# Rows' root on VectorE and ScalarE, first pieces in halves and two products interleaved at the start of a Fourier and SwiGLU kernel

## The chip, the cores and the metric

One core of one Trainium2 chip. The metric is the device time of one execution in microseconds (us). Beside three timed runs there is one profiled execution, whose trace gives every instruction of the five engines (PE is TensorE, with PEld for its weight loads; DVE is VectorE; ACT is ScalarE; POOL is GpSimd; SP is SyncE, which only issues DMAs) and the DMA traffic. Times in the trace count from the start of its span.

## What is computed

```python
def reference(A_x, A_dft_seq_re, A_dft_seq_im, A_dft_hid_re, A_dft_hid_im, B_x, B_w_gate, B_w_up, B_w_down):
    xn = layernorm(A_x)                       # S=2048 rows, D=640
    a = einsum("bsd,ed->bse", xn, dft_hid_re)
    b = einsum("bsd,ed->bse", xn, dft_hid_im)
    s = einsum("ts,bse->bte", dft_seq_re, a) - einsum("ts,bse->bte", dft_seq_im, b)
    g = silu((silu(xn @ w_gate) * (xn @ w_up)) @ w_down)      # F=1536
    return A_x + s * g
```

All is float32.

## The kernel before

**Arithmetic.** Each float32 product is done as three matmuls in the reduced float32r format (`mm3`, lines 199 to 205): an operand is split into a high part (ScalarE, `high`, line 182) and a low part, the remainder (VectorE, `low`, lines 187 and 189), and high x high, high x low and low x high are added in PSUM. The three lines 203, 204, 205 are those three matmuls; the first needs both high parts, the second also the low part of the moving operand, the third the low part of the stationary one. Nearly all of TensorE's time is in them, 4290 matmuls.

**Stages.** First the Fourier transform along the sequence, four times (`seq(0)` to `seq(3)`: two pairs of column blocks, real and imaginary), then twice the transform along the hidden dimension (`hid`), gate and up (`gate_up`) and down (`down`). The sequence products use a Strassen scheme on quarters of the DFT matrix and of the normalised rows. In `seq` (line 526) the products are run in the order p1, d, p5, p2, p6, p3, p7, p4 for the first one. Each product has four blocks g = 0 to 3; a block takes one piece of 128x1024 of the DFT matrix (two tiles of 128x512) as moving operand S, and two row tiles of the normalised input as stationary operand T. A block of p1 and of p2 has 18 matmuls (two banks of p and a third for a fifth block of columns, called d1 or d2), a block of d has 6 (only the fifth column block, with the quarter a21), one of the others 12.

**Names used below.** x0 to x15 are the row tiles of x (128x640); x0 to x7 are loaded by SP for p1, x8 to x15 by GpSimd's queue for p2 (`load_x`, line 401). c0 to c3 are the four pieces of quarter 11 that p1 reads; R0 to R3 those of quarter 21 that d reads (`load`, line 546, on SP). Into R0 to R3 GpSimd's queue then adds quarter 22, with DMAs that accumulate (`accumulate`, line 551), which gives p5's operands; then quarter 11, for p6, and quarter 12, for p3. An accumulate may only start when the split of what was there before has been read.

**Normalisation of rows** (only `seq(0)`, `layer_norm`, line 403). For each pair of row tiles: two `bn_stats` per tile and one `bn_aggr` on VectorE (lines 410 and 412), then the inverse root of the variance, refined by one Newton step, on tiles of 128x2 (lines 420 to 435), then on ScalarE one activation per tile that scales and shifts it in place (line 440). For the first pair the small operations run on VectorE, with ScalarE's square root; for the seven other pairs on GpSimd, with `pow`: eight operations each, in GpSimd's queue, which also issues the accumulating DMAs and the loads of x8 to x15. After that T of the pair is split: high parts of 128x512 and 128x256 for the two p tiles and the d tile, low parts the same. p5, p6 and p4 use sums of row tiles made on VectorE (lines 459 and 478).

**What sets the order.** Nothing is scheduled at run time: `Plan` records every operation with a planned time, which is that of the product that needs it less a lead (`prod`), and raises it to what its reads and writes allow. All operations are then sorted by this time, and each engine executes its own in that order, waiting where a semaphore says so. The leads of the first sequence product stand in `LEAD` (line 522). `Plan.place` gives each buffer a place in two arenas by the planned lifetimes. An SP or GpSimd queue also waits, before its ninth DMA, for the first one's landing, and so on.

Ahead of the first product 16 matmuls on zeros (line 987) run on TensorE.

Of the kernel before, what the change touches and what calls it, by code (L numbers as in the profile page):

```python
# [13 lines left out]
P = 128  # L14
# [12 lines left out]
class Plan:  # L27
# [43 lines left out]
    def place(self, limits):  # L71
# [9 lines left out]
        for arena, limit in limits.items():  # L81
# [13 lines left out]
            where |= min(found, key=lambda f: f[0])[1]  # L95
# [3 lines left out]
    def fit(mine, limit, pauses):  # L99

        placed, where, cost = [], {}, 0.0
        for n, size, ta, ia, tb, ib in mine:
# [17 lines left out]
            for a, e, xa, ja, xb, jb in near:  # L120
                if a < o + size and o < e:
                    cost += max(0.0, 5 - (ta - xb if ta >= xa else xa - tb)) ** 2
            placed.append((o, o + size, ta, ia, tb, ib))
        return cost, where
# [3 lines left out]
def tile_fnet_swiglu(  # L128
# [27 lines left out]
    sm = one.tile([P, 6, NS], F32, name="sm")  # L156
# [246 lines left out]
    def layer_norm(k0, n, lead, root, stats, small):  # L403
# [4 lines left out]
        for k in range(k0, k0 + n):  # L408
            for h in range(2):
                pl.prod(stats, lambda k=k, h=h: nc.vector.bn_stats(  # L410
                    bst[:, k % 2, h], raw(xn, k * D + h * 320, 320)), [(xn, k)], [("bst", k % 2, h)])
            pl.prod(stats, lambda k=k: nc.vector.bn_aggr(
                mv[:, k], bst[:, k % 2].rearrange("p a b -> p (a b)")),
                [("bst", k % 2, 0), ("bst", k % 2, 1)], [("mv", k)])
        v, y, t, mr, nm, power = (sm[:, i, k0:k0 + n] for i in range(6))
        r = rowst[:, 0, NS + k0:NS + k0 + n]
        key = ("sm", k0)
        if small is nc.vector:
            ops = [
                lambda: small.tensor_scalar(v, mv[:, k0:k0 + n, 1], EPS, 1.0, op0=ALU.add, op1=ALU.mult),  # L420
                lambda: nc.scalar.activation(t, v, AF.Sqrt),
                lambda: small.reciprocal(y, t),
            ]
        else:
            ops = [
                lambda: small.tensor_scalar(v, mv[:, k0:k0 + n, 1], EPS, 1.0, op0=ALU.add, op1=ALU.mult),  # L426
                lambda: small.tensor_tensor(y, v, power, op=ALU.pow),  # L427
            ]
        ops += [
            lambda: small.tensor_scalar(nm, mv[:, k0:k0 + n, 0], -1.0, 0.0, op0=ALU.mult, op1=ALU.add),  # L430
            lambda: small.tensor_tensor(t, v, y, op=ALU.mult),
            lambda: small.tensor_tensor(t, t, y, op=ALU.mult),
            lambda: small.tensor_scalar(t, t, -0.5, 1.5, op0=ALU.mult, op1=ALU.add),
            lambda: small.tensor_tensor(r, y, t, op=ALU.mult),
            lambda: small.tensor_tensor(mr, nm, r, op=ALU.mult),
        ]
        for fn in ops:
            pl.prod(root, fn, [("mv", k) for k in range(k0, k0 + n)], [key])
        for k in range(k0, k0 + n):
            pl.prod(lead, lambda k=k: nc.scalar.activation(  # L440
                raw(xn, k * D, D), raw(xn, k * D, D), AF.Identity, bias=sm[:, 3, k:k + 1], scale=rowst[:, 0, NS + k:NS + k + 1]),
# [45 lines left out]
    def down_operands():  # L487

        for g in range(2):
# [32 lines left out]
    LEAD = {"S": (10, 8), "T": (14, 13, 11), "p1": (5.5, 0.6), "p5": (4.5, 2.5), "p2": (8, 6),  # L522
            ("d", 0): (8.8, 4.5), ("d", 1): (9.7, 5.7), ("d", 2): (8, 6.4), ("d", 3): (9.2, 7.7),
            "Tp1": (0, 2, 0), "Td1": (0, 2, 0), "Tp5": (5.5, 4.5, 2.6), "Tp2": (0, 6, 4), "Td2": (0, 6, 4)}

    def seq(k):
# [4 lines left out]
        top = {}  # L531
# [11 lines left out]
        def load(q, g, lead):  # L543
            seq.n += 1
            name = pl.buf(("c", seq.n), "raw", 2 * TC)
            pl.prod(lead, lambda: nc.sync.dma_start(wide(raw(name)), source(q, g)), [], [(name, 0)])
            return name

        def accumulate(name, q, g, lead):

            pl.prod(lead, lambda: nc.gpsimd.dma_start(wide(raw(name)), source(q, g), accum_op=ALU.add), [], [(name, 0)], 8)  # L551
# [5 lines left out]
        def operand(p, g, name):  # L557
            s = pl.buf(("S", k, p, g), "hl", 4 * TC)
            high, low = LEAD.get((p, g), LEAD.get(p, LEAD["S"])) if fresh else LEAD["S"]
            split(high, s, 2 * TC, lambda: raw(name), [(name, 0)], low_lead=low)  # L560
            return s

        def right_operand(p, g, per):

            width = P if p[0] == "d" else 256
            sums, high, low = LEAD.get("T" + p, LEAD["T"]) if fresh else LEAD["T"]
            view, keys = right(p, per * g // 4, sums)
            name = pl.buf(("T", k, p, per * g), "hl", 2 * per * width)
            at = per * g % 4
            split(high, name, per * width, lambda: view(at, per), keys[at:at + per] if len(keys) > 1 else keys,  # L570
                  scale=-1.0 if p == "p1" else None, low_lead=low)
            for i in range(per):
                top[p, per * g + i] = name, per, i, width

        def tw(p, kk, e):
            name, per, i, width = top[p, kk]
            return lambda part: hl(name, part, i * width + e * P, P)

        def run(p, left, banks, direct=None):

            per = 6 * (len(banks) + (direct is not None))
            operands = []
            rights = ([p] if banks else []) + ([f"d{direct[1]}"] if direct else [])
            start = pl.now
            for g in range(4):
                pl.now = start + g * per * MM
                operands.append(left(g))
                for r in rights:
                    few = 2 if fresh and r in ("p1", "d1", "p2", "d2") else 4
                    if (r, 2 * g) not in top:  # L590
                        right_operand(r, 2 * g // few, few)
            pl.now = start
            for g, s in enumerate(operands):
                todo = []
                reads = both(s)
                for kk in (2 * g, 2 * g + 1):
                    m = lambda i, kk=kk, s=s: hl(s, i, kk % 2 * TC, TC)
# [431 lines left out]
```

## Time and profile before

| what | us |
|---|---|
| three timed runs: median (lowest to highest) | 998.49 (998.20 to 999.53) |
| profiled execution, its own time | 999.22 |
| its span, first to last instruction | 997.2 |
| first matmul of p1, first of p5 | 11.93, 42.40 |
| mean granted clock of TensorE over the span | 0.994 |

The page gives busy time per engine and groups of instructions by source line. A line such as L182 or L187 is that of a helper, and stands for all splits; which operand a row belongs to follows from its place in the engine's order. `hl<-raw` is a split, `raw<-in_cs` a load or accumulate of the DFT matrix, `raw<-in_x` a load of rows. Rows of the timeline are: start, duration, engine, line, operation, shape, count, and in brackets how long the engine stood before and what ended that. A matmul of 512 columns shows 0.39 us, but they overlap; one starts every 0.226 us.

### The profile page before, as it was taken

To read this page: it belongs to the slowest core of one execution; us is meant where nothing else is said; L and a number is where in the kernel's file an instruction comes from. 1 tells how busy PE (TensorE), PEld (TensorE's weight loads), DVE (VectorE), ACT (ScalarE), POOL (GpSimd) and SP (SyncE) were. 2 spreads that over 40 slices of the span, in tenths; PEclk is the share of its full clock that TensorE was granted. 3 is DMA by queue.
4 is the path that set the end of the run, shared out by engine and by line. 5 is a ranking of instruction groups with operands and counts; after the bars stand their busy time and mean duration, and the time that the engine had idled before them with its cause. 6 is when DMAs were issued, how large, how long until landed. Compare 5 with 4: busy or idle time off the path is not lost.

```text
span 997.2 us, 11758 instructions
## 1 busy us (share of the span) xinstructions
PE 981.2 (98%) x4306; PEld 806.8 (81%) x4306; DVE 708.3 (71%) x912; ACT 499.4 (50%) x708; POOL 123.4 (12%) x204
## 2 busy tenths in 40 slices
PE   7899999999999999999999999999999999999998
PEld 4688888888888888888888888888888888887887
DVE  6787767946785686466678887787668666666686
ACT  6676554655375454424655555434434544445342
POOL 4760211001101010001111110000010100000000
PEclk9899999999999999999999999999999999999999
DMA  9879667656765776833545534489950311205683
GB/s 343 208 158 251 237 154 158 211 181 147 158 211 200 169 171 212 281 137 118 184 144 217 203 145 159 172 293 356 333 170 28 124 36 53 79 1 188 228 281 126
DMA packets 71193, 180.09 MB, mean 181 GB/s; under 512 B 6432, under 2 KB 22048, under 8 KB 71136
## 3 DMA queue, kind: packets, MB, share of 16 engines
q1 hardware_dynamic: 56064, 122.96, 36.3%
q0 software_dynamic: 15072, 56.39, 20.9%
q8 instruction: 33, 0.54, 0.2%
q14 instruction: 24, 0.20, 0.1%
HBM read 145.75 MB, written 33.57 MB: 180 GB/s over the span
## 4 chain that ended last, share of the span: by engine, by line
PE 89%; POOL 3%; DMA 3%; DVE 3%; issue 2%; ACT 1%; SPq 0%; POOLq 0%; DVEq 0%; ACTq 0%
PE ps L203 30%; PE ps L205 29%; PE ps L204 29%; DVE hl L187 1%; DMA p_dram<-raw 1%; POOL raw L551 1%; DMA raw<-in_cs 1%; DMA raw<-in_x 1%; DVE bst L410 1%; POOL sm L427 1%; ACT hl L182 0%; POOL sm L426 0%; POOL raw L401 0%; DVE raw L459 0%; POOL sm L430 0%
## 5 line engine op out<-in xcount | busy, mean ns | idle before, releaser
L203 PE MATMUL ps<-hl 128*128 128x512 f32 (+1 forms) x1430 | 558.3, 390 | 9.1 <-ACT hl L182 8.1
L204 PE MATMUL ps<-hl 128*128 128x512 f32 (+1 forms) x1430 | 557.5, 390 | 0.2 <-DVE hl L187 0.2
L205 PE MATMUL ps<-hl 128*128 128x512 f32 (+1 forms) x1430 | 557.5, 390 | 0.2 <-DVE hl L187 0.2
L182 ACT ACTIVATE hl<-raw 128x1024 fp32r<-128x1024 f32 (+6 forms) x504 | 375.6, 794 | 265.0 <-PE ps L204 63.6
L187 DVE TENSOR_TENSOR hl<-raw,hl 128x1024 fp32r<-128x1024 f32 (+5 forms) x434 | 395.0, 941 | 145.5 <-ACT hl L182 70.3
L203 PEld LDWEIGHTS ps<-hl 128*128 128x128 f32 x1430 | 269.6, 189 | 67.0 <-ACT hl L182 9.0
L204 PEld LDWEIGHTS ps<-hl 128*128 128x128 f32 x1430 | 269.6, 189 | 57.0 <-DVE hl L187 1.7
L205 PEld LDWEIGHTS ps<-hl 128*128 128x128 f32 x1430 | 269.3, 188 | 57.1 <-DVE hl L189 0.9
L228 ACT ACTIVATE raw<-ps 128x512 f32<-128x512 f32 (+1 forms) x122 | 80.3, 676 | 127.8 <-PE ps L205 105.5
L233 DVE TENSOR_TENSOR raw<-ps,raw 128x512 f32<-128x512 f32 (+1 forms) x90 | 71.5, 796 | 55.9 <-PE ps L205 54.9
L898 DVE TENSOR_TENSOR raw<-raw 128x512 f32<-128x512 f32 x24 | 16.6, 692 | 49.6 <-ACT raw L897 49.6
L551 POOL DMA_DIRECT2D raw<-in_cs x40 | 35.4, 940 | 112.5 <-DVE raw L554 86.0
L189 DVE SCALAR_TENSOR_TENSOR hl<-raw,hl 128x256 fp32r<-128x256 f32 (+5 forms) x70 | 43.5, 621 | 6.8 <-ACT hl L182 5.9
L811 DVE TENSOR_TENSOR raw<-raw 128x256 f32<-128x256 f32 (+1 forms) x96 | 47.8, 519 | 0.0
L960 POOL DMA_DIRECT2D out<-raw x10 | 6.7, 671 | 303.1 <-ACT hl L182 187.5
L615 POOL DMA_DIRECT2D p_dram<-raw x24 | 17.2, 745 | 194.4 <-DVE raw L233 145.5
L554 DVE TENSOR_TENSOR raw<-raw 128x1024 f32<-128x1024 f32 x24 | 29.3, 1219 | 9.7 <-DMA raw<-in_cs 9.7
L736 POOL DMA_DIRECT2D y_dram<-raw x20 | 10.9, 546 | 132.5 <-ACT raw L228 132.1
L876 ACT ACTIVATE raw<-raw 128x512 f32<-128x512 f32 x24 | 15.2, 633 | 23.2 <-DVE raw L233 23.2
L514 POOL DMA_DIRECT2D d_p<-hl x28 | 15.1, 541 | 79.9 <-ACT hl L182 66.3
L897 ACT ACTIVATE raw<-ps 128x512 f32<-128x512 f32 x24 | 14.3, 594 | 19.7 <-PE ps L205 19.7
L764 DVE TENSOR_TENSOR raw<-raw 128x1024 f32<-128x1024 f32 (+1 forms) x24 | 23.8, 1041 | 0.0
(47 smaller groups left out, 191.4 us busy)
## 6 DMA issues: line engine op xcount, KB each, us to landing
raw<-in_cs SPq DMA_DIRECT2D x76, 512.0 KB, 6.0
hl<-d_p SPq DMA_DIRECT2D x56, 384.0 KB, 4.9
raw<-in_cs POOLq DMA_DIRECT2D x40, 512.0 KB, 8.0
raw<-in_wb SPq DMA_DIRECT2D x24, 640.0 KB, 4.2
d_p<-hl POOLq DMA_DIRECT2D x28, 384.0 KB, 2.9
raw<-p_dram SPq DMA_DIRECT2D x8, 1280.0 KB, 8.9
p_dram<-raw POOLq DMA_DIRECT2D x16, 512.0 KB, 5.4
raw<-in_hd SPq DMA_DIRECT2D x20, 320.0 KB, 7.7
```

The lines of the kernel that those rows point to most:

```text
L182: nc.scalar.activation(like(hl(dst, 0, a, n)), src(), AF.Copy, scale=1.0 if scale is None else scale)
L187: nc.vector.tensor_tensor(lo, src(), hi, op=ALU.subtract)
L189: nc.vector.scalar_tensor_tensor(lo, src(), scale, hi, op0=ALU.mult, op1=ALU.subtract)
L203: nc.tensor.matmul(o, w(0), m(0), start=first, stop=False, skip_group_check=True)
L204: nc.tensor.matmul(o, w(0), m(1), start=False, stop=False, skip_group_check=True)
L205: nc.tensor.matmul(o, w(1), m(0), start=False, stop=True, skip_group_check=True)
L228: pl.post(lambda: nc.scalar.activation(wide(raw(dst, a, n)), pair(b), AF.Copy), pkeys(b), [(dst, a)], after)
L233: pl.post(lambda: nc.vector.tensor_tensor(wide(raw(dst, a, n)), pair(b), wide(raw(other)), op=op), [*pkeys(b), (other, 0)], [(dst, a)], after)
L551: pl.prod(lead, lambda: nc.gpsimd.dma_start(wide(raw(name)), source(q, g), accum_op=ALU.add), [], [(name, 0)], 8)
L554: pl.prod(lead, lambda: nc.vector.tensor_tensor(raw(dst), raw(dst), raw(src), op=ALU.add), [(src, 0)], [(dst, 0)])
L764: pl.prod(46 - 6 * q - 2 * i - half, lambda i=i, op=op, part=part, rows=rows, nb=nb: nc.vector.tensor_tensor(part(), part(), raw(rows, i * ...
L811: pl.prod(lead, lambda o=o, a=a, b=b, op=op: nc.vector.tensor_tensor(o(), a(), b(), op=op), [(w, 0)], [(c, lead)])
```

## The change

1. **Root.** For all eight pairs: ScalarE takes the square root of the variance with EPS as bias (`sm[:, 3]`, set by GpSimd's memset), VectorE then does five operations, each waiting for the one before: the reciprocal, three `scalar_tensor_tensor` for the Newton step, one for minus mean times root. GpSimd has no part in it any more.
2. **First pieces in halves.** c0 is loaded and split as two tiles of 128x512 (`load_tiles`, `halves`). The row tiles of p1's first three blocks are split one by one (`few` is 1) right after their normalisation: a 256-wide part for p1 and a 128-wide one for d1, high and low each; p1's products are issued per half block, so that each half waits only for its own operands.
3. **Interleaving.** In the first sequence product p1 and d run as one, in the order p1 0, p1 1, d 0, p1 2, d 1, p1 3, d 2, d 3. The loads follow that order: on SP's queue x0, x1, half of c0, x2, x3, the other half, c1, x4, x5, c2, R0, x6, x7, c3, R1, R2, R3.
4. **Warm-up** of 22 matmuls instead of 16.
5. New leads for the first sequence product. The loads of x8 to x15 have lead 17 instead of 20, the pieces of p2 14 instead of 17. In GpSimd's queue the order becomes: accumulate into R0, R1, R2, R3, load x8, x9, x10, x11, accumulate into R0, R1, load x12, x13, and so on; before it was R0, R1, x8, x9, R2, R3, x10 to x13, R0, then a root, and so on.
6. `Plan.place` tries up to 24 further orders per arena, with the buffers first whose neighbours in time are near; places in both arenas move throughout the kernel. The order of instructions behind the first sequence product stays.

```diff
@@ -92,13 +92,23 @@
-            where |= min(found, key=lambda f: f[0])[1]
+            best = min(found, key=lambda f: f[0])
+            order, last = best[3], best
+            for _ in range(24):
+                hurt = sorted((n for n in last[2] if last[2][n] > 9), key=lambda n: -last[2][n])
+                moved = {n: i for i, n in enumerate(hurt[:6])}
+                order = sorted(order, key=lambda m: moved.get(m[0], 99))
+                last = next((f for f in (self.fit(order, limit, pauses[a:]) for a in range(len(pauses))) if f), None)
+                if last is None:
+                    break
+                best = min(best, last, key=lambda f: f[0])
+            where |= best[1]
...
@@ -400,45 +410,36 @@
-        v, y, t, mr, nm, power = (sm[:, i, k0:k0 + n] for i in range(6))
+        y, t, mr = (sm[:, i, k0:k0 + n] for i in range(3))
+        mean, var = (mv[:, k0:k0 + n, i] for i in range(2))
         r = rowst[:, 0, NS + k0:NS + k0 + n]
         key = ("sm", k0)
-        if small is nc.vector:
-            ops = [
-                lambda: small.tensor_scalar(v, mv[:, k0:k0 + n, 1], EPS, 1.0, op0=ALU.add, op1=ALU.mult),
-                lambda: nc.scalar.activation(t, v, AF.Sqrt),
-                lambda: small.reciprocal(y, t),
-            ]
-        else:
-            ops = [
-                lambda: small.tensor_scalar(v, mv[:, k0:k0 + n, 1], EPS, 1.0, op0=ALU.add, op1=ALU.mult),
-                lambda: small.tensor_tensor(y, v, power, op=ALU.pow),
-            ]
-        ops += [
-            lambda: small.tensor_scalar(nm, mv[:, k0:k0 + n, 0], -1.0, 0.0, op0=ALU.mult, op1=ALU.add),
-            lambda: small.tensor_tensor(t, v, y, op=ALU.mult),
-            lambda: small.tensor_tensor(t, t, y, op=ALU.mult),
-            lambda: small.tensor_scalar(t, t, -0.5, 1.5, op0=ALU.mult, op1=ALU.add),
-            lambda: small.tensor_tensor(r, y, t, op=ALU.mult),
-            lambda: small.tensor_tensor(mr, nm, r, op=ALU.mult),
+        stt = nc.vector.scalar_tensor_tensor
+        ops = [
+            lambda: nc.scalar.activation(t, var, AF.Sqrt, bias=sm[:, 3, :1]),
+            lambda: nc.vector.reciprocal(y, t),
+            lambda: stt(t, var, EPS, y, op0=ALU.add, op1=ALU.mult),
+            lambda: stt(t, t, -0.5, y, op0=ALU.mult, op1=ALU.mult),
+            lambda: stt(r, t, 1.5, y, op0=ALU.add, op1=ALU.mult),
+            lambda: stt(mr, mean, -1.0, r, op0=ALU.mult, op1=ALU.mult),
         ]
...
@@ -519,16 +520,22 @@
-    LEAD = {"S": (10, 8), "T": (14, 13, 11), "p1": (5.5, 0.6), "p5": (4.5, 2.5), "p2": (8, 6),
-            ("d", 0): (8.8, 4.5), ("d", 1): (9.7, 5.7), ("d", 2): (8, 6.4), ("d", 3): (9.2, 7.7),
-            "Tp1": (0, 2, 0), "Td1": (0, 2, 0), "Tp5": (5.5, 4.5, 2.6), "Tp2": (0, 6, 4), "Td2": (0, 6, 4)}
+    LEAD = {("xn", 0): ((2.6, 1.0), (6, 6), (7, 7)), ("xn", 1): ((3.9, 2.0), (4.31, 4.22), (6.2, 4.32)),
+            ("xn", 2): ((3.9, 3), (5, 4.5), (6.8, 6.1)), ("xn", 3): ((3.9, 3), (6.87, 6.7), (9.8, 7.9)), ("xn", 4): ((7.5, 7.5), (11, 10.9), (12, 12)),
+            ("S", 0): (2.8, 2.2), ("S", 1): (0.4, 0.2), ("Tp1", 0): (0, 1.8, 0.6), ("Td1", 0): (0, 1.7, 0.5),
+            ("Tp1", 1): (0, 2.6, 2.15), ("Td1", 1): (0, 2.5, 2.1), ("Tp1", 2): (0, 2.6, 1.5), ("Td1", 2): (0, 2.5, 1.4),
+            ("Tp1", 3): (0, 3.2, 2.95), ("Td1", 3): (0, 3.15, 2.94), ("p1", 1): (3.94, 3),
+            ("Tp1", 4): (0, 3.8, 2.6), ("Td1", 4): (0, 3.7, 2.55), ("Tp1", 5): (0, 4.9, 3.5), ("Td1", 5): (0, 4.8, 3.4),
+            "S": (10, 8), "T": (14, 13, 11), "p1": (5.15, 4.9), "p5": (4.5, 2.5), "p2": (8, 6),
+            ("d", 0): (4.95, 4.85), ("d", 1): (5.5, 5.1), ("d", 2): (8.7, 8.4), ("d", 3): (7.8, 6.8),
+            "Tp1": (0, 2.6, 1.5), "Td1": (0, 2.5, 1.4), "Tp5": (5.5, 4.5, 2.6), "Tp2": (0, 6, 4), "Td2": (0, 6, 4)}
...
+        def load_tiles(q, leads):
+
+            seq.n += 1
+            name = pl.buf(("c", seq.n), "raw", 2 * TC)
+            for i in range(2):
+                pl.prod(leads[i], lambda i=i: nc.sync.dma_start(raw(name, i * TC, TC), source(q, 0)[:, i]), [], [(name, i)])
+            return name
...
+        def halves(p, g):
+            return (0, 1) if fresh and (p, g) == ("p1", 0) else (0,)
...
+                        few = 4 if not fresh or r not in ("p1", "d1", "p2", "d2") else 2 if g > 2 or r[1] == "2" else 1
...
+                if fresh and p == "p1":
+                    for step in zip(steps, reads):
+                        product(*step)
+                else:
+                    product(steps[0] + steps[1], list(dict.fromkeys(reads[0] + reads[1])))
...
             if fresh:
                 for kk in (8 + 2 * g, 9 + 2 * g):
-                    load_x(kk, 20, nc.gpsimd)
-                layer_norm(8 + 2 * g, 2, 7.5, 11, 12, nc.gpsimd)
-            return operand("p2", g, load(12, g, 17))
+                    load_x(kk, 17, nc.gpsimd)
+                layer_norm(8 + 2 * g, 2, *LEAD["xn", 4])
+            return operand("p2", g, load(12, g, 14 if fresh else 17))
...
-        run("p1", p1, b2, (1, 1))
+        first_two = ("p1", p1, b2, (1, 1)), ("d", d, (), (2, 1))
+        if fresh:
+            run(*first_two, order=((0, 0), (0, 1), (1, 0), (0, 2), (1, 1), (0, 3), (1, 2), (1, 3)))
+        else:
+            run(first_two[0])
         s1 = copy("s1", b2)
-        run("d", d, (), (2, 1))
+        if not fresh:
+            run(first_two[1])
...
-    nc.gpsimd.memset(sm[:, 5], -0.5)
+    nc.gpsimd.memset(sm[:, 3], EPS)
...
-            for _ in range(16):
+            for _ in range(22):
                 nc.tensor.matmul(warm, z[:, :P], z, start=True, stop=True)
```

More of the change, by code (lines that the diff above doesn't have):

```diff
@@ new lines, in layer_norm @@
+        ops = [
[5 more added lines that the diff above has]
+            lambda: stt(mr, mean, -1.0, r, op0=ALU.mult, op1=ALU.mult),
+        ]
+        for i, fn in enumerate(ops):
+            pl.prod(root[i > 0], fn, [("mv", k) for k in range(k0, k0 + n)], [key])
@@ L530, in seq @@
         first = {}
-        top = {}
+        top, made = {}, set()
         fresh = k == 0
@@ L559, in operand @@
             high, low = LEAD.get((p, g), LEAD.get(p, LEAD["S"])) if fresh else LEAD["S"]
-            split(high, s, 2 * TC, lambda: raw(name), [(name, 0)], low_lead=low)
-            return s
+            for i, sub in enumerate(halves(p, g)):
+                n = 2 * TC // len(halves(p, g))
+                lead = (high, low) if n > TC else LEAD["S", i]
+                split(lead[0], s, n, lambda i=i, n=n: raw(name, i * n, n), [(name, j) for j in range(2) if n > TC or j == i],
+                      i * n, sub=sub, low_lead=lead[1])
@@ L572, in right_operand @@
             for i in range(per):
-                top[p, per * g + i] = name, per, i, width
+                top[p, per * g + i] = name, sub, (sub + i) * width
         def tw(p, kk, e):
[L576 to L583, printed above, removed]
-            start = pl.now
[L585 to L591, printed above, removed]
+            name, _, at = top[p, kk]
```

98 lines of the change are left out of this document (59 added, 39 removed).

## The prediction

> **What bounds the kernel now.** First the page and the waits of PE over the whole span (engine, line, who it waited for: total us, times, longest).
>
> ```profile
> span 997.2 us, 11758 instructions
> PE 981.2 (98%) x4306; PEld 806.8 (81%) x4306; DVE 708.3 (71%) x912; ACT 499.4 (50%) x708; POOL 123.4 (12%) x204
> ```
> ```profile
> PE ps L203 <- ACT hl L182: 8.1, 2, 4.6
> ```
>
> TensorE is the bound; what can be won are its pauses, of which the first blocks' operands make the longest. Next the busy time by stretch (PE, PEld, DVE, ACT, POOL with counts, then granted clock, DMA share, GB/s).
>
> ```profile
> 3.40:67.00 63.60, 55.26 (x215) 41.77 (x214) 51.58 (x96) 42.78 (x56) 41.31 (x74) 0.92 0.86 246
> 8.60:11.90 3.30, 0.00 (x0) 0.00 (x0) 2.46 (x7) 3.27 (x5) 0.30 (x1) 1.00 1.03 416
> 12.00:15.40 3.40, 3.40 (x7) 2.26 (x8) 3.33 (x9) 1.18 (x3) 2.83 (x8) 0.50 1.03 407
> 25.60:29.00 3.40, 0.96 (x5) 0.46 (x3) 1.04 (x1) 1.44 (x2) 2.71 (x6) 1.00 0.13 53
> 29.00:36.00 7.00, 6.00 (x14) 4.68 (x15) 4.64 (x6) 5.12 (x7) 5.10 (x9) 0.51 0.91 155
> ...
> 250.00:500.00 250.00, 250.00 (x1105) 207.05 (x1104) 170.36 (x183) 122.06 (x159) 23.98 (x34) 1.00 0.61 184
> 120.60:992.90 872.30, 871.61 (x3859) 721.45 (x3858) 614.05 (x776) 424.65 (x617) 70.79 (x109) 1.00 0.54 174
> ```
>
> At full clock a matmul takes 250/1105 = 0.226 us. From 120.6 us on PE lacks 872.30 - 871.61 = 0.7 us: nothing to win or lose but that. All else lies in the first 110 us: the start, one pause at 26, and after each a stretch at clock 0.50. The timeline of PE shows the warm-up and the first matmul, then the pause, then the first matmul of p5, which is the end of p1 and d.
>
> ```profile
> 2.28 5.02 PE L987 MATMUL ps<-z 128*128 128x512 bf16 x16 [2.28 <-ACT z L980]
> 11.93 0.80 PE L203 MATMUL ps<-hl 128*128 128x512 f32 x1 [4.63 <-ACT hl L182]
> ```
> ```profile
> 26.17 0.39 PE L205 MATMUL ps<-hl 128*128 128x512 f32 x1
> 30.00 0.79 PE L203 MATMUL ps<-hl 128*128 128x512 f32 x1 [3.44 <-ACT hl L182]
> ```
> ```profile
> 42.40 0.39 PE L203 MATMUL ps<-hl 128*128 128x512 f32 x1
> ```
>
> The second thing to see is the first row's VectorE: 51.58 us busy in 63.6, only 12.0 idle. And PE lives from hand to mouth on it. The last block of p2 starts at 65.90; its third matmul needs the low part of x14 and x15, which VectorE ends at 66.66 (65.97 plus 0.69 of a 512-wide one; the three in that row end with p6's first low part at 68.1). p3's third block waits too, for a piece that DMAs accumulate. Timelines of PE, then of VectorE:
>
> ```profile
> 66.71 0.51 PE L205 MATMUL ps<-hl 128*128 128x512 f32 x1 [0.20 <-DVE hl L187]
> ```
> ```profile
> 87.38 0.50 PE L204 MATMUL ps<-hl 128*128 128x512 f32 x1 [0.15 <-DVE hl L187]
> ```
> ```profile
> 65.97 2.16 DVE L187 TENSOR_TENSOR hl<-raw,hl 128x512 fp32r<-128x512 f32 x3
> ```
>
> So time won in the first block stays won only if VectorE is also through p2's operands earlier.
>
> **The change, part by part.** Durations, by line and form in the first 110 us:
>
> ```profile
> L187 DVE TENSOR_TENSOR hl<-raw,hl 128x1024 fp32r<-128x1024 f32 x42 | 49.5, 1216 | 11.9 <-ACT hl L182 11.9
> L410 DVE BATCH_NORM_STATS2 bst<-raw 128x6 f32<-128x320 f32 x32 | 13.8, 472 | 5.6 <-DMA raw<-in_x 5.6
> ...
> L187 DVE TENSOR_TENSOR hl<-raw,hl 128x256 fp32r<-128x256 f32 x8 | 3.4, 419 | 0.0
> ```
> ```profile
> L427 POOL TENSOR_TENSOR sm<-sm 128x2 f32<-128x2 f32 x7 | 8.7, 1243 | 0.6
> ```
> ```profile
> 6.62 0.17 DVE L433 TENSOR_SCALAR sm<-sm 128x2 f32<-128x2 f32 x1
> 6.83 0.16 DVE L434 TENSOR_TENSOR rowst<-sm 128x2 f32<-128x2 f32 x1
> 7.02 0.16 DVE L435 TENSOR_TENSOR sm<-sm,rowst 128x2 f32<-128x2 f32 x1
> ```
>
> *Root.* Seven groups leave GpSimd, where one operation alone took 1.24 us on average. On VectorE five dependent ones, started 0.2 us apart, make 1.0; seven groups add 6.7 us to VectorE's queue (7 x 1.0, less 0.3 that the first group gets shorter). ScalarE's square root takes 0.20, hidden in ScalarE's idle time, but it stands in that queue and waits for the statistics; what is behind it (high parts) waits along.
>
> ```profile
> 5.80 0.20 ACT L421 ACTIVATE sm<-sm 128x2 f32<-128x2 f32 x1 [3.58 <-DVE sm L420]
> 8.54 1.06 ACT L182 ACTIVATE hl<-raw 128x1024 fp32r<-128x1024 f32 x1 [2.54 <-DMA raw<-in_cs]
> 9.50 1.72 ACT L440 ACTIVATE raw<-raw,sm,rowst 128x640 f32<-128x640 f32 x2
> ```
>
> *Halves.* Six narrow pairs of low parts replace three wide ones, two halves one piece: with about 0.1 us overlap between neighbours, 0.58 per pair (0.33 for 256, 0.25 taken for 128, which no row has: between 0.16 of a tiny one and 0.33) against 0.94 for the wide pair, so 3 x 0.22 + 0.1 = 0.8, and the waits between them. VectorE gets 7.5 us more, perhaps 8.2, before p2 is done.
>
> *First matmul.* From issue to landing x1 (issued 1.18) takes 3.1 us, the first c piece (1.64) 6.9, x2 (2.11) 7.2:
>
> ```profile
> raw<-in_x SPq DMA_DIRECT2D x1, 320.0 KB, 3.1
> ```
> ```profile
> raw<-in_cs SPq DMA_DIRECT2D x1, 512.0 KB, 6.9
> ```
> ```profile
> raw<-in_x SPq DMA_DIRECT2D x1, 320.0 KB, 7.2
> ```
>
> They land at 4.2, 8.5 and 9.3. Half a piece lands between 6.4 (half way from 4.2 to 8.5) and 7.9 (the other half saves 0.26 MB at the 416 GB/s of the second row above, 0.6 us). I take 6.4, since those first transfers are slow throughout; 1.5 us more would change nothing behind the third matmul. Then come a high split, one normalisation (0.9) and a narrow high part: PE starts at 8.4 instead of 11.93. The six further warm-up matmuls take at most 6 x 5.02/16 = 1.9 us of an engine that would stand, and end at about 8.4. The third matmul waits: the low part of x0 stands in VectorE's queue behind the statistics of x2, which lands at 8.7 (0.6 us fewer bytes ahead of it): 8.7 + 1.04 + 0.33 = 10.1. The second half's third matmul needs x1's low part, which stands behind x3's statistics, the half's own low part and the second root: 13.3. Seven matmuls later, at 14.9, block 0 is done.
>
> *The interleaving.* d's first block fits before p1's third; its operand's load moves ahead of x6, x7 and c3 on SP's queue, which land some 1.3 us later, still long before they are read. VectorE from x2 to the low part of R3 (d's last operand) holds 6 x 1.04 of statistics, 3 roots, 7 low parts of 1024 at 1.13, 6 narrow pairs, and 1.55 of wider ones: 6.2 + 3.0 + 7.9 + 3.5 + 1.6 = 22.2, from 8.7 to 30.9, with 1.6 us of small waits 32.5. Before, R3's low part ended at 33.6:
>
> ```profile
> 31.23 2.36 DVE L187 TENSOR_TENSOR hl<-raw,hl 128x1024 fp32r<-128x1024 f32 x2 [0.23 <-ACT hl L182]
> ```
>
> PE waits for the high parts of x4 (20 to 22.5) and of x6 and x7 (28 to 29.6), but p1 and d are through at about 37 instead of 42.4.
>
> *What is late next.* In GpSimd's queue x8 to x11 are now issued **behind** all four accumulates into R0 to R3 (lead 17 instead of 20); before, x8 and x9 went out third and fourth:
>
> ```profile
> 27.93 2.05 POOL L551 DMA_DIRECT2D raw<-in_cs  x2 [0.41 <-issue]
> 29.28 1.82 POOL L401 DMA_DIRECT2D raw<-in_x  x2
> 32.76 0.90 POOL L551 DMA_DIRECT2D raw<-in_cs  x1 [1.66 <-DVE hl L187]
> ```
> ```profile
> raw<-in_cs POOLq DMA_DIRECT2D x1, 512.0 KB, 5.8
> ```
> ```profile
> raw<-in_x POOLq DMA_DIRECT2D x1, 320.0 KB, 8.9
> ```
>
> The last two rows are the accumulate of 27.93, 5.8 us to land with the engines free, and x8's gather of 29.28, landed at 38.2. R3's accumulate waits for its low part, 32.5, lands at 38.4; x8 behind it at 39.4, x9 0.8 later. VectorE has by then made p5's first sum and, once ScalarE has split that, two low parts (32.5 + 1.2 + 1.1 + 2.2 = 37.0), and stands 2.4 us before x8's statistics; behind these wait p5's second sum, a root and the low part of R1 which p5's second block needs: 39.4 + 2.1 + 1.1 + 1.0 + 1.2 = 44.8. Before:
>
> ```profile
> 41.41 1.22 DVE L187 TENSOR_TENSOR hl<-raw,hl 128x1024 fp32r<-128x1024 f32 x1
> ```
>
> that is 42.6. The five us won are gone: PE stands from 39.8 to 44.8. From there to x14's low part VectorE holds 8 parts of 1024 at 1.13, 2 sums at 1.17, 3 pairs of statistics at 2.08, 3 roots, 3 pairs of a 512 and a 256 at 0.94, and a 512 at 0.69: 9.0 + 2.3 + 6.2 + 3.0 + 2.8 + 0.7 = 24.0, with 0.6 of waits 69.4, against 66.7. PE leaves p2 2.7 us later than before.
>
> Of this 0.4 to 0.6 comes back where p3 waited before (87.38): its accumulates into R0 to R3 start when p6's first low part is done, 70.9 instead of 68.1, but no longer stand behind the two that GpSimd issued late after its last root; the third block's operand is ready at 89.2, PE there at 89.4. Behind it all engines have room. **Sum: +2.7 - 0.5, taken as +2.1 us.** The span becomes 999.3; the profiled execution took 999.22, 2.0 more than its span and 0.7 above the median of 998.49, from which I count: **1000.6 us**. Moved buffers in the rest I take at nothing, within the 0.7 us above.
>
> **The rivals.**
> 1. *The gathers come early.* If x8 is there when VectorE wants it, at 37, its 2.4 us go: 998.2. For it: the transfers of x take 0.8 each. Against it: the order of GpSimd's queue.
> 2. *VectorE keeps up*, ending faster. Of 12.0 us idle in the first row, 7.5 to 8.2 could take up all that is added, and the work starts earlier. The price turns at R3's low part: done by 28 instead of 32.5, x8 lands by 35 and p2 ends 4 us before its old time; p3's accumulates, started that much earlier, allow it. 998.5 - 4 = 994.5. Against it: 22.2 us of operations stand between x2 and that part.
> 3. *Cold clock on top.* A pause with 0.96 us of work in 3.4 was followed by 0.51 over 7 us (rows above): 14 matmuls, where 31 fit, a loss near 3 us. PE's new pause of 5 us would bring the same. From 44.8 PE needs 108 x 0.226 = 24.4 us to the end of p2 at 73.1, so 3.9 us hide it; two such stretches, 6 us, end 2 us later: 1002.7. [...]
>
> **How the numbers follow.** A measurement of this kernel tells about 0.2% (2.0 us) from no change. The forecast's mechanism has 0.62; its size is known to some 1.5 us either way (R3's part between 30.9 and 33.5, x8 behind it), so 0.34 of it lies above 2.0 and 0.28 below. Rival 1 has 0.11 (same), rival 2 0.13 (faster), rival 3 0.14 (slower). Slower 0.48, same 0.39, faster 0.13. The range leaves out rival 2 and the forecast's and rival 3's ends above 1003.8; below it reaches to rival 1 less the same 1.5 us, 996.6.
>
> **What would show it.** Right: first matmul at 8 to 9; p1 and d done at 35 to 38; VectorE idle before x8's statistics, then PE idle before p5's second block until 43 to 46; p6 starts after 71. Wrong: x8 landing before 37, or R3's low part before 30; then the gain of the first block lives on. If p6 starts before 69 the forecast's sign is wrong.

## The result, and the profile after

The changed kernel takes 1002.22 us (median of 10 runs, 1000.74 to 1002.88); the kernel before took 999.50 beside it (10 runs, 998.20 to 1000.22). The ratio is 1.0027, with a 95% interval of 1.0017 to 1.0037: slower by 0.27%, 2.7 us; 2.1 had been forecast. The forecast time, 1000.6 us, lies 1.6 below: 1.0 of that is the kernel before, which had been counted at 998.49, and 0.6 is the sum. In the profiled execution (1002.36 us, span 1000.6) the splits are L192 (high), L197 and L199 (low), the three matmuls L213 to L215, the loads of rows L411, the accumulates L566 and the root L431 to L436.

First the busy time by stretch (PE, PEld, DVE, ACT, POOL, then granted clock, DMA share, GB/s):

```profile
3.40:67.00 63.60, 55.01 (x211) 40.59 (x210) 54.08 (x131) 41.92 (x66) 13.40 (x18) 0.92 0.91 257
12.00:15.40 3.40, 2.71 (x12) 2.28 (x13) 3.33 (x10) 3.00 (x7) 0.00 (x0) 1.00 1.03 408
39.30:44.80 5.50, 0.21 (x1) 0.00 (x0) 5.09 (x14) 3.05 (x4) 0.00 (x0) 0.90 0.67 151
44.80:50.10 5.30, 5.25 (x12) 4.12 (x13) 5.09 (x15) 5.30 (x9) 2.52 (x4) 0.50 0.61 107
123.10:995.40 872.30, 871.61 (x3859) 721.29 (x3857) 613.00 (x775) 424.30 (x617) 70.82 (x109) 1.00 0.54 174
```

The last row is the test that nothing else moved: from the second sequence product on, PE is busy 871.61 of 872.30 us, to the hundredth what it was before. All that changed up to the last matmul lies ahead of it. In the first row PE got no busier (55.01 against 55.26) although its first matmul comes 3.2 us earlier: a pause at the start was traded for one at 39.3, and the waits of PE name it.

```profile
PE ps L214 <- DVE hl L197: 5.3, 1, 5.3
PE ps L213 <- ACT hl L192: 2.0, 1, 2.0
```

The timeline of PE has the first matmul, p5's first, the end of that wait (p5's second block), the two waits in p2 and p6's first:

```profile
8.76 0.58 PE L213 MATMUL ps<-hl 128*128 128x512 f32 x1
...
36.40 0.39 PE L213 MATMUL ps<-hl 128*128 128x512 f32 x1
...
44.85 0.79 PE L214 MATMUL ps<-hl 128*128 128x512 f32 x1 [5.34 <-DVE hl L197]
64.85 0.50 PE L215 MATMUL ps<-hl 128*128 128x512 f32 x1 [0.50 <-DVE hl L197]
69.78 0.50 PE L215 MATMUL ps<-hl 128*128 128x512 f32 x1 [0.47 <-DVE hl L197]
...
73.56 0.39 PE L213 MATMUL ps<-hl 128*128 128x512 f32 x1
```

p5 starts 6.0 us earlier than before, p6 3.05 later. What lies between is seen in GpSimd's queue (the accumulate into R3, then the gathers of x8 to x11) and on VectorE (the low part of R3; two low parts of p5; the statistics of x8, for which it stood 2.97 us):

```profile
31.95 0.86 POOL L566 DMA_DIRECT2D raw<-in_cs  x1 [2.31 <-DVE hl L197]
32.49 2.50 POOL L411 DMA_DIRECT2D raw<-in_x  x4
```

```profile
30.43 1.22 DVE L197 TENSOR_TENSOR hl<-raw,hl 128x1024 fp32r<-128x1024 f32 x1 [0.23 <-ACT hl L192]
...
33.92 2.36 DVE L197 TENSOR_TENSOR hl<-raw,hl 128x1024 fp32r<-128x1024 f32 x2 [1.13 <-ACT hl L192]
39.26 0.89 DVE L420 BATCH_NORM_STATS2 bst<-raw 128x6 f32<-128x320 f32 x2 [2.97 <-DMA raw<-in_x]
...
69.04 3.29 DVE L197 TENSOR_TENSOR hl<-raw,hl 128x512 fp32r<-128x512 f32 x4
```

The last row begins with the low part of x14 and x15: 69.04 plus 0.69 is 69.73, and PE's wait ends there.

The stages, by the starts of their first matmuls in the profiles of all kernels of this study (us); at 0.226 us each the 120 matmuls of p5 and p2 are 27.1 us without a pause, the 96 of p6 and p3 21.7:

| kernel | p1 | p5 | p6 | p5 and p2 | p6 and p3 | last matmul | time against before |
|---|---|---|---|---|---|---|---|
| before | 11.93 | 42.40 | 70.51 | 28.1 | 22.3 | 992.76 | 1 |
| after | 8.76 | 36.40 | 73.56 | 37.2 | 21.8 | 995.21 | 1.0027 |
| e1 | 8.85 | 36.68 | 70.45 | 33.8 | 21.8 | 991.98 | 0.9997 |
| e2 | 8.49 | 36.31 | 74.90 | 38.6 | 22.9 | 997.78 | 1.0068 |
| e3 | 9.38 | 37.20 | 74.00 | 36.8 | 23.6 | 997.57 | 1.0035 |
| e4 | 8.70 | 36.51 | 74.19 | 37.7 | 21.8 | 995.88 | 1.0030 |
| e5 | 9.15 | 36.48 | 68.36 | 31.9 | 22.6 | 990.93 | 0.9982 |
| e6 | 8.57 | 36.38 | 72.86 | 36.5 | 21.8 | 994.28 | 1.0017 |
| e8 | 12.21 | 38.78 | 72.85 | 34.1 | 21.8 | 994.62 | 1.0022 |
| e9 | 12.53 | 42.15 | 73.88 | 31.7 | 22.4 | 996.25 | 1.0019 |
| e10 | 9.24 | 36.49 | 70.25 | 33.8 | 22.6 | 992.88 | 0.9991 |
| e11 | 9.60 | 36.33 | 69.13 | 32.8 | 22.7 | 991.86 | 0.9996 |
| e12 | 9.60 | 36.48 | 71.82 | 35.3 | 21.8 | 992.86 | 1.0003 |
| e13 | 9.20 | 36.57 | 67.34 | 30.8 | 23.4 | 990.74 | 0.9980 |

So the start of p1 and d wins some six us (5.2 to 6.1) in every kernel that has the whole of it, and the column "p5 and p2" takes them back: 9.0 us in the changed kernel.

### The profile page after: what moved, and what is told of

Its sections match the earlier page's. It is cut to its first block, busy times and chain, and to the rows that moved or that the text cites. A ratio compares the mean times of both kernels' runs of the same rounds, so it can differ in the third digit from the quotient of the medians.

```text
span 1000.6 us, 11738 instructions
## 1 busy us (share of the span) xinstructions
PE 983.2 (98%) x4312; PEld 807.3 (81%) x4312; DVE 713.7 (71%) x951; ACT 501.3 (50%) x722; POOL 95.5 (10%) x148
## 4 chain that ended last, share of the span: by engine, by line
PE 88%; DVE 3%; issue 3%; DMA 2%; ACT 2%; POOL 1%; SPq 0%; DVEq 0%; POOLq 0%; ACTq 0%
PE ps L213 29%; PE ps L215 29%; PE ps L214 29%; DVE hl L197 2%; DMA p_dram<-raw 1%; ACT hl L192 1%; POOL raw L566 1%; DMA raw<-in_x 1%; ACT raw L441 1%; DMA raw<-in_cs 0%; DVE bst L420 0%; DVE raw L460 0%; DVE raw L243 0%; DVE raw L479 0%; DVE mv L422 0%
## 5 line engine op out<-in xcount | busy, mean ns | idle before, releaser
L213 PE MATMUL ps<-hl 128*128 128x512 f32 (+1 forms) x1430 | 557.5, 390 | 3.0 <-ACT hl L192 2.0
L215 PE MATMUL ps<-hl 128*128 128x512 f32 (+1 forms) x1430 | 557.3, 390 | 1.7 <-DVE hl L197 1.0
L192 ACT ACTIVATE hl<-raw 128x1024 fp32r<-128x1024 f32 (+7 forms) x511 | 376.3, 785 | 239.2 <-PE ps L215 48.4
L197 DVE TENSOR_TENSOR hl<-raw,hl 128x1024 fp32r<-128x1024 f32 (+5 forms) x438 | 395.1, 935 | 125.7 <-ACT hl L192 97.8
L213 PEld LDWEIGHTS ps<-hl 128*128 128x128 f32 x1430 | 269.4, 188 | 61.1 <-ACT hl L192 2.9
L215 PEld LDWEIGHTS ps<-hl 128*128 128x128 f32 x1430 | 269.4, 188 | 59.0 <-DVE hl L199 1.8
L566 POOL DMA_DIRECT2D raw<-in_cs x40 | 35.1, 933 | 161.3 <-DVE raw L569 90.4
L199 DVE SCALAR_TENSOR_TENSOR hl<-raw,hl 128x384 fp32r<-128x384 f32 (+5 forms) x73 | 43.9, 601 | 5.1 <-PE ps L215 2.7
L922 ACT ACTIVATE raw<-raw 128x512 f32<-128x512 f32 x24 | 15.2, 632 | 22.6 <-DVE raw L243 22.5
```

Of the source, the lines that this page charges most:

```text
L192: nc.scalar.activation(like(hl(dst, 0, a, n)), src(), AF.Copy, scale=1.0 if scale is None else scale)
L197: nc.vector.tensor_tensor(lo, src(), hi, op=ALU.subtract)
L199: nc.vector.scalar_tensor_tensor(lo, src(), scale, hi, op0=ALU.mult, op1=ALU.subtract)
L213: nc.tensor.matmul(o, w(0), m(0), start=first, stop=False, skip_group_check=True)
L215: nc.tensor.matmul(o, w(1), m(0), start=False, stop=True, skip_group_check=True)
```

## The experiments

The theory (**G**): the gain is lost at x8, which is gathered behind the accumulates. The rivals: VectorE's added work (**V**), and the half clock behind the pause (**K**). The edits are to the changed kernel, unless it says the kernel before. A pause of PE that stands below without its line is counted from one matmul's start to the next, less the 0.226 us of one; the bracket in a line is some 0.2 us shorter.

### e1: x8 and x9 through SP's queue

```diff
-                    load_x(kk, 17, nc.gpsimd)
+                    load_x(kk, *((17, nc.gpsimd) if g else (36, nc.sync)))
```

> x8 and x9 are fetched through SP's queue behind the last piece of d instead of through GpSimd's behind the accumulates; nothing else moves. Theory G (the late gathers cost the gain of the first block): VectorE no longer stands 2.97 us before x8's statistics, p5's second block goes on at 41.9 instead of 44.85, p6 starts at 70.6 instead of 73.56, and the time falls by 2.5 to 3 us, to 999.4, level with the kernel before. Rival V (VectorE's added work holds p2 back whatever the gathers do): p6 starts above 72.5 and the time stays above 1001.5. Rival K (the clock at half speed behind the pause is what costs): the pause shrinks to 2.5 us, the half-speed stretch stays, p6 starts at 72.5 to 73 and the time is 1001 to 1001.7.

Measured: 998.98 us, ratio 0.9997 (0.9988 to 1.0006); p6 at 70.45. VectorE goes from p5's two low parts to x8's statistics without a stop:

```profile
34.19 2.36 DVE L197 TENSOR_TENSOR hl<-raw,hl 128x1024 fp32r<-128x1024 f32 x2 [1.13 <-ACT hl L192]
36.47 0.88 DVE L420 BATCH_NORM_STATS2 bst<-raw 128x6 f32<-128x320 f32 x2
```

G holds, to 0.15 us at p6: two transfers on another queue are worth 3.1 us. But the result is only level with the kernel before. The six us of the first block are still eaten, now by what VectorE does in p5 and p2 (33.8 us against 28.1): from these two low parts to x14's low part it waits only 1.1 us in all, 0.36 at most at once, and that part ends at 66.60, for 66.66 in the kernel before. So V isn't false; it is what is left.

### e2 and e3: the roots of x8 to x15 on GpSimd again

```diff
+        if k0 >= 8:
+            v, power = (sm[:, i, k0:k0 + n] for i in (4, 5))
+            small = nc.gpsimd
+            ops = [
+                lambda: small.tensor_scalar(v, var, EPS, 1.0, op0=ALU.add, op1=ALU.mult),
+                lambda: small.tensor_tensor(y, v, power, op=ALU.pow),
...
+            ]
```

The eight operations are those of the kernel before. e3 has the edit of e1 too.

> The roots of x8 to x15 go back to GpSimd's eight operations per group; those of x0 to x7 stay in five fused steps. Theory G: x8 still comes at 39.2 and p5's second block goes on at 43.8 instead of 44.85; VectorE then has 4 us less up to x14's low part, which comes to 65.7, and PE, 36 products of p5 less one and 72 of p2 behind 43.8 with 2.5 us lost at half clock, ends p2 at 70.7 instead of 73.56: the time falls by 2.9 us, to 999.3. Rival V: with VectorE's work gone the whole loss is gone and more, 4 us, 998.2 or less. If GpSimd's steps come too late for the normalisations, nothing is won: 1002 or more.

> Both edits: x8 and x9 early through SP's queue, roots of x8 to x15 on GpSimd. Theory G with the work of VectorE behind it: p5's second block goes on at 40.8, PE ends p2 at 65.2 with a warm clock or 67.7 with the half-speed stretch, VectorE ends x14's low part at 62.7; the time falls by 5.9 to 8.4 us against the changed kernel, to 994 to 996.3, faster than both. If the two edits remove the same loss and no more, 999.3.

Measured: e2 1006.92 (1.0068, 1.0055 to 1.0081), e3 1002.43 (1.0035, 1.0022 to 1.0047). G's and V's expectations fell for both. What came true for e2 is the last one, that GpSimd's steps come too late (1002 or more). In e2 the roots stand in GpSimd's queue ahead of the gathers; the gather of x14 and x15 goes out at 52.34, where it went at 50.16 in the changed kernel:

```profile
47.52 0.53 POOL L442 TENSOR_SCALAR sm<-mv 128x2 f32<-128x2 f32 x1
48.13 1.58 POOL L443 TENSOR_TENSOR sm<-sm 128x2 f32<-128x2 f32 x1
...
51.72 0.94 POOL L579 DMA_DIRECT2D raw<-in_cs  x1 [0.33 <-issue]
52.34 1.43 POOL L411 DMA_DIRECT2D raw<-in_x  x2
```

VectorE, relieved of its roots, is there earlier and stands for x12, x14 and x15, 4.6 us in all:

```profile
52.66 0.89 DVE L420 BATCH_NORM_STATS2 bst<-raw 128x6 f32<-128x320 f32 x2 [2.58 <-DMA raw<-in_x]
...
58.36 0.89 DVE L420 BATCH_NORM_STATS2 bst<-raw 128x6 f32<-128x320 f32 x2 [1.52 <-DMA raw<-in_x]
...
59.99 0.89 DVE L420 BATCH_NORM_STATS2 bst<-raw 128x6 f32<-128x320 f32 x2 [0.50 <-DMA raw<-in_x]
```

The last root then takes GpSimd from 61.21 to 67.46, so that PE stands in p2's last block; two accumulates behind it in the same queue go out at 67.8 instead of 53.3, and p6 and p3 take 22.9 us. In e3 VectorE stands 2.19, 1.83 and 0.81 us for the same three tiles. The profiled execution is the shortest of e2's five (1004.41); the rest of its distance is not in a trace.

### e4: no pause for the clock

```diff
+                if fresh and (p, g) == ("p5", 1):
+                    pl.step(0, lambda: [nc.tensor.matmul(ps[:, 2], z[:, :P], z, start=True, stop=True) for _ in range(20)],
+                            [], [("ps", 2)])
```

> Twenty matmuls on zeros into a bank that nobody uses at that time stand ahead of p5's second block, so that PE is busy in the pause; nothing else moves. Theory G: the granted clock stays at 1.00 behind the pause (0.50 in 44.8 to 50.1 before), p5 ends 2.4 us earlier, and PE then waits for VectorE in p2, whose order is unchanged: p6 starts 0 to 0.3 us earlier, time 1001.9 to 1002.2. Rival K: p6 starts 2.4 us earlier and the time is 999.8.

Measured: 1002.81 us, 1.0030 (1.0018 to 1.0041), as the changed kernel. The two stretches of the pause and behind it:

```profile
39.30:44.80 5.50, 4.66 (x22) 2.00 (x21) 3.54 (x11) 2.40 (x4) 0.00 (x0) 1.00 0.74 169
44.80:50.10 5.30, 3.34 (x13) 2.47 (x14) 5.16 (x12) 5.30 (x9) 2.01 (x3) 1.00 0.45 74
```

The clock stayed at 1.00 where it was 0.50, and nothing came of it: PE is busy only 3.34 of the 5.3 us and waits for VectorE instead. p6 even starts 0.6 us later, because x9 landed later in this run (VectorE stood 1.93 and 1.78 us for x8 and x9). K is out: here half speed was free, since PE had to wait anyway.

### e5: all eight gathers through SP, roots on GpSimd

```diff
-                    load_x(kk, 17, nc.gpsimd)
+                    load_x(kk, 36 + 4.1 * g, nc.sync)
```

and the edit of e2.

> All of x8 to x15 come early through SP's queue, and the roots of x8 to x15 are GpSimd's, so that no transfer is issued behind a root. In the run with both edits x12 and x14 were issued behind GpSimd's roots and VectorE stood 2.2, 1.8 and 0.8 us for them. Theory G2 (that alone spoiled the GpSimd roots): those 4.8 us go, x14's low part comes by 64, PE ends p2 at 66.5 to 67.5 (70.4 with x8 and x9 early alone): 995 to 996.5, faster than the kernel before by 0.3 to 0.4%. Rival L (GpSimd's root is too long a chain, 5 to 6 us from statistics to normalisation): the normalisations come late by themselves, PE still waits in p2's blocks and the time stays at 998.5 or above.

Measured: 997.69 us, 0.9982 (0.9973 to 0.9991): faster than both kernels, by less than expected, with p6 at 68.36 instead of 66.5 to 67.5. The missing us is a wait of 2.6 in p5's third block, whose operand is an accumulated piece. The DMA issues between 26 and 33 us (KB, median us from issue to landing), of e5 and then of e1:

```profile
raw<-in_cs POOLq DMA_DIRECT2D x3, 512.0 KB, 10.8
raw<-in_cs SPq DMA_DIRECT2D x2, 512.0 KB, 17.4
```

```profile
raw<-in_cs POOLq DMA_DIRECT2D x3, 512.0 KB, 6.7
```

With eight gathers ahead of them on SP's queue, p2's pieces, which nobody needs before p2, travel beside the accumulates into R1 to R3, and these take 10.8 us instead of 6.7. How the two queues share the DMA engines isn't shown by these times.

### e6 and e12: four tiles to a root

```diff
-                layer_norm(8 + 2 * g, 2, *LEAD["xn", 4])
+                if g % 2 == 0:
+                    layer_norm(8 + 2 * g, 4, (7.5, 7.5, 3.4, 3.4), (7.8, 7.7), (12, 12, 7.9, 7.9))
```

e6 has the loads of e5, e12 those of e10 (in the order in which x10 to x15 should have gone there).

> All of x8 to x15 come early through SP's queue; their roots stay on VectorE, but two groups of four tiles take the place of four groups of two, ten instructions instead of twenty and two waits for the square root instead of four. Theory V (VectorE's instructions for the root are what is left of the loss): 2 us less on VectorE before p2's last operand, p6 starts at 68.3 instead of 70.4, time 997 (998.98 with x8 and x9 early alone). Rival: once the gathers are early VectorE isn't last any more and nothing moves: 998.6 to 999.3.

> The roots of x8 to x15 in two groups of four on VectorE once more, but with x8 and x9 early through SP and x10 to x15 through GpSimd behind the accumulate into R3, so that nothing travels beside the accumulates. Theory V with the transfers out of the way: 2 us less on VectorE than with x8 and x9 early alone (998.98): 997 to 997.6. If the delay of the first run with groups of four (1001.01) was the waiting for a second pair's statistics and not the transfers, PE stands 3 us and more in p5's last block again and the time is 1000 or above.

Measured: e6 1001.01 us, 1.0017 (1.0008 to 1.0026); e12 999.71, 1.0003 (0.9994 to 1.0012). Both expectations of e6 fell. In e12 the pause in p5's last block came as the second one has it (2.95 us), with a time 0.3 us below its 1000. Ten instructions fewer on VectorE were no gain: e6 is slower than e1, and e12 can't be told from it, with p6 1.4 us later. (Both also load x10 to x15 otherwise than e1, so this comparison isn't of the roots alone; the wait below is.) ScalarE's square root now waits for the statistics of x10 and x11, and p5's last high parts stand behind it. ScalarE, then PE of e12:

```profile
45.09 0.30 ACT L431 ACTIVATE sm<-mv,sm 128x4 f32<-128x4 f32 x1 [2.60 <-DVE mv L422]
46.42 1.73 ACT L441 ACTIVATE raw<-raw,sm,rowst 128x640 f32<-128x640 f32 x2 [1.03 <-DVE sm L436]
48.06 2.81 ACT L192 ACTIVATE hl<-raw 128x1024 fp32r<-128x1024 f32 x4
```

```profile
49.15 0.80 PE L213 MATMUL ps<-hl 128*128 128x512 f32 x1 [2.95 <-ACT hl L192]
```

The count of instructions was the wrong measure; this pause comes from the place of one that waits in an in-order queue. It says nothing on what VectorE's 2 us less would bring alone.

### e8: the kernel before with VectorE's root alone

```diff
-        v, y, t, mr, nm, power = (sm[:, i, k0:k0 + n] for i in range(6))
-        if small is nc.vector:
...
+        stt = nc.vector.scalar_tensor_tensor
+        ops = [
+            lambda: nc.scalar.activation(t, var, AF.Sqrt, bias=sm[:, 5, :1]),
...
```

> The kernel before with one part of the change alone: the root of all groups in five fused steps on VectorE; gathers, order, pieces and warm-up as before. The prediction's price for it is 6.7 us more of VectorE before p2's last operand, of which its idle time behind the first block (some 3.5 us) takes up a part: p6 starts 2 to 4 us later than 70.5 and the time is 1001.3 to 1003.5. Rival (a root on VectorE is quicker at hand than GpSimd's eight operations, and pays for itself): p6 at 70.5 or earlier, time 999.5 or less.

Measured: 1001.41 us, 1.0022 (1.0014 to 1.0031); p6 at 72.85, 2.3 later. Both are at the low end of what was expected for the root's price. p5 starts 3.6 us earlier (38.78), since the first normalisations no longer wait for GpSimd, and p5 and p2 take 6.0 us longer: from p5's first low parts at 35.94 on VectorE waits only 1.5 us in all, and x14's low part ends at 69.00, 2.3 us later than in the kernel before.

### e9: the kernel before with early gathers

```diff
-                    load_x(kk, 20, nc.gpsimd)
+                    load_x(kk, 36 + 4.1 * g, nc.sync)
```

> The kernel before with x8 to x15 early through SP's queue and nothing else. Its VectorE never waits for x8 to x15 by its timeline, and PE's pauses from 42.4 on are short, so theory G expects no difference: 998.7 to 999.9. If accumulates and gathers on GpSimd's queue held one another up in that kernel too, p3's wait at 87.4 goes and the time is 998.5 or less.

Measured: 1001.12 us, 1.0019 (1.0010 to 1.0028), which neither side had expected. It is what e5 shows, without anything to win: p2's pieces travel beside the accumulates, ScalarE stands 5.90 us for R0's and VectorE behind it 5.37. So eight early gathers are no gain of their own; e1's gain was the changed kernel's own late gathers. ScalarE, then VectorE:

```profile
38.67 2.01 ACT L182 ACTIVATE hl<-raw 128x1024 fp32r<-128x1024 f32 x2 [5.90 <-DMA raw<-in_cs]
```

```profile
40.71 2.36 DVE L187 TENSOR_TENSOR hl<-raw,hl 128x1024 fp32r<-128x1024 f32 x2 [5.37 <-ACT hl L182]
```

### e10, e11 and e13: two gathers on SP, six on GpSimd ahead of the roots

```diff
-                    load_x(kk, 17, nc.gpsimd)
+                    load_x(kk, *((12.9 + 4.1 * g, nc.gpsimd) if g else (36, nc.sync)))
```

and the edit of e2; e13 has 4 for 4.1. In e11 the statistics of x10 and x11 have lead 11.2 instead of 12.

> x8 and x9 early through SP's queue, x10 to x15 in GpSimd's queue in one row behind the last accumulate into R3 and ahead of every root, roots of x8 to x15 on GpSimd. With all eight early through SP, p2's own pieces were in flight beside the accumulates into R1 to R3, which landed at 35.9, 39.6 and 43.5 instead of 33.5, 36.0 and 38.4, and PE stood 2.6 us before p5's third block. Theory G3 (these accumulates were held up by the other transfers): they land by 33.6, 36.1 and 38.6, the 2.6 us shrink to 1.5 or less, and the time is 996.3 to 996.9 (997.69 with all eight through SP). Rival: the 2.6 us are VectorE's own work (statistics of x10 and x11 ahead of that operand), and the time stays at 997.5 or above.

> As the run before, and the statistics of x10 and x11 stand behind the low part that p5's third block needs, not ahead of it. If VectorE's order is what is left of that pause, it goes (1.5 us or less of PE), and the time falls by 1 to 1.5 us more, to 995 to 995.8, unless p2's later operands then come late by the same; in that case it equals the run before.

> As the run with x10 to x15 in one row on GpSimd's queue and roots of x8 to x15 on GpSimd, but the row goes out as x10, x11, x12 to x15; in that run it had gone out as x14, x15, x12, x13, x10, x11, x10 and x11 landed last, at 43.7 and 44.4, VectorE stood 1.77 us for them and PE 3.4 us at p5's third block. Theory G: x10 lands at 39.2 and x11 at 40, that wait of 1.77 goes, PE's pause at p5's third block is 1.6, p2 starts at 50.4 and p7 at 89.5; time 995.8 to 997.2, the fastest of all. Rival (the order of these six doesn't matter, GpSimd's roots and p3's accumulates set the end): 998 to 998.6 as in that run.

Measured: e10 998.53 us, 0.9991 (0.9982 to 1.0000), e11 998.98, 0.9996 (0.9988 to 1.0005), e13 997.50, 0.9980 (0.9971 to 0.9989). The accumulates landed at 34.0, 36.5 and 39.0 in e10, 0.4 us after what G3 had said and 2 to 4.5 us before e5's, so G3 was right about them. The time is on the rival's side (997.5 or above), for a reason that neither had: the factor 4.1 sent the six gathers out in the wrong order, x10 and x11 last, and VectorE stood for them:

```profile
43.67 0.89 DVE L420 BATCH_NORM_STATS2 bst<-raw 128x6 f32<-128x320 f32 x2 [1.77 <-DMA raw<-in_x]
```

In e11 PE's pause moved from p5's third block to its last one (0.9 and 1.0 us) and the time didn't fall. e13, with the order mended, has p5's pause at 1.54 as expected, p2 at 50.50 (50.4 expected) and p6 at 67.34, 6.2 us before the changed kernel. So of e5's 2.6 us there the late accumulates had made about 1.1; in e13 the statistics of x10 and x11 (41.89 to 43.9) stand on VectorE ahead of the low part that ends the pause. Its time is 0.3 us above what was expected, since p6 and p3 take 23.4 us: p3's pieces come only 4.4 us earlier than in the changed kernel, PE waits for them, and ScalarE ahead of it for the DMAs. PE, then ScalarE of e13:

```profile
85.17 0.50 PE L214 MATMUL ps<-hl 128*128 128x512 f32 x1 [0.76 <-DVE hl L197]
```

```profile
77.68 1.06 ACT L192 ACTIVATE hl<-raw 128x1024 fp32r<-128x1024 f32 x1 [4.15 <-DMA raw<-in_cs]
82.80 2.01 ACT L192 ACTIVATE hl<-raw 128x1024 fp32r<-128x1024 f32 x2 [4.06 <-DMA raw<-in_cs]
```

One of the six accumulates there landed 4.2 us behind the one ahead of it, the others 2.5 to 3.0; why is open.

e13 and e5 are faster than the kernel before by 0.2%, with intervals that leave out 1 by 0.1%, and than the changed one by 0.4 to 0.5%; they cannot be told from each other.

## Why the prediction was right, point by point

- **The bound.** All that moved is in the first 110 us; right.
- **Root.** Forecast 6.7 us more on VectorE and a loss from it: e8 alone costs 2.2 us: right. e13, which takes the roots of x8 to x15 off VectorE again, has p6 3.1 us before e1 (ratio 0.9980 against 0.9997), but it also gathers x10 to x15 earlier, and e2 and e3, with the same roots and late gathers, are slower; what the roots alone give there is not shown. That the square root stands in ScalarE's queue was costed at little; in the changed kernel that holds (waits of 0.36), in e12 it made a pause of 2.95.
- **First matmul** 8.76 for 8.4, second half's third matmul 12.69 for 13.3, d and p1 through at 36.40 for 37: right. The low part of x0 was no wait (PE's third matmul at 9.40 for 10.1): x2 landed at 7.4 and not 8.7.
- **The pause for x6 and x7** (28 to 29.6) did not come in this execution; a stretch at half clock ate it (last section).
- **What is late next.** R3's low part at 31.65 for 32.5, x8 at 39.26 for 39.4, VectorE idle 2.97 us for 2.4, p5's second block at 44.85 for 44.8. That x8 is met so closely is in part luck: the accumulate into R3 went out 0.55 us earlier than forecast (31.95) and took 6.47 us to land instead of 5.8. This step carried the sign, and e1 confirms it: without the late gathers the loss is gone. Rival 1, the same thing as a chance, had been put at 998.2; e1 measured 998.98.
- **x14's low part** at 69.73 for 69.4; PE leaves p2 3.05 us later for 2.7. The term that was too small is the 0.6 of waits in that stretch: VectorE waited 1.1 us there (0.36, 0.36, 0.19 and 0.22), twice 0.36 of it for ScalarE's square root.
- **What p3 gives back** was 0.51 us (3.05 at p6, 2.54 at p7) for 0.5. From there on the loss stays near 2.5, to 2.45 at the last matmul.
- **Rival 3** was half right: behind the pause PE ran at 0.50 for 5.3 us, but the forecast had found that 3.9 us of cover hide one such stretch, and it was hidden; in e4, without it, PE waited for VectorE instead and the time was the same.
- **Rival 2** asked for R3's low part by 28; it came at 31.65.
- The sum was 0.3 to 0.6 us short. 2.45 is PE's last matmul, the rest to 2.7 lies behind it or within what runs differ by: from last matmul to the end the profiles of this study show 4.4 to 5.4 us.

Not tried alone: the halves, the interleaving, the longer warm-up, the later loads of p2's pieces and the moved places of the buffers.

## What to carry to other kernels

A gain at the start of an in-order pipeline is only kept if the next engine in line has room for it (here 6.0 us won at p5 were 3.05 lost at p6): ask what each queue is made to do earlier, and what then stands ahead of it. A transfer that another engine needs next does not belong behind DMAs that wait for results (x8 and x9 moved from there: p6 3.1 us earlier, e1), nor behind a chain of small operations on the issuing engine (VectorE stood 4.6 us for three tiles, e2), nor beside bulk loads that nobody needs yet (10.8 us to land instead of 6.7, e5). Count queue positions of instructions that wait before counting instructions (ten fewer, and a pause of 2.95 us, e12).

## What the runs showed of the hardware

Eleven profiles (the changed kernel and those with edits to it) have the same instructions on PE, VectorE and ScalarE up to the pause of 2.2 us near 20 us. In four (the changed kernel, e1, e2, e6) PE then ran at half clock for about 3.4 us, in seven it did not. The changed kernel, then e13:

```profile
19.60:23.00 3.40, 1.36 (x6) 0.76 (x5) 2.83 (x13) 2.35 (x4) 0.00 (x0) 1.00 1.05 381
23.20:26.60 3.40, 3.40 (x10) 2.64 (x9) 3.23 (x11) 3.33 (x6) 0.07 (x1) 0.51 1.03 294
```

```profile
19.60:23.00 3.40, 1.40 (x6) 0.79 (x5) 2.83 (x12) 2.19 (x4) 0.00 (x0) 1.00 1.05 383
23.20:26.60 3.40, 3.40 (x16) 2.79 (x16) 3.23 (x12) 3.33 (x6) 0.00 (x0) 1.00 1.03 285
```

So a pause of that length does not decide by itself: of the 3.40 us from 19.60 PE is busy 1.36 to 1.39 in the four and 1.38 to 1.42 in the seven, and in the 3.40 us from 23.20 it starts 10 matmuls in the four, 16 or 17 in the seven.

In the first 60 us of the changed kernel's trace the first record of the granted clock begins at 6.17, although the warm-up starts at 2.29, and the clock changes at 23.24, 26.65, 43.72 and 50.55: 5, 1, 5 and 2 times 3.41 us from one to the next. In the kernel before, the first record begins at 5.14 (warm-up at 2.28) and the changes are at 11.96, 15.38, 29.03 and 35.85: 2, 1, 4 and 2 times 3.41 us. In the 3.41 us ahead of each change to 0.50 PE was busy 1.37 and 0.00 us in the changed kernel, 0.03 and 0.94 in the kernel before. What decided between the four and the seven isn't shown.

It made no difference to the start of p5: where the clock stayed up PE waited some 1.55 us for x6 and x7 instead (of the 2.00 us from 27.40 it was busy 0.59 to 0.61 in six of the seven and 1.20 in e3, for 2.00 in the four), and p5 started between 36.3 and 36.7 in ten of the eleven (37.2 in e3).
